# An attention and feed-forward kernel: pair 0's short pieces loaded alone, readers of later loads planned behind the landing with a margin, early squares and normalizations allowed on DVE

## The chip, the cores and the metric

The kernel runs on one core of one Trainium2 chip. The metric is the device time of one execution in microseconds (us); the kernel before takes 449.25 us, the median of three runs (449.05 to 450.95). The core's engines have queues of their own that run in order: TensorE (PE; its weight loads are shown as PEld), VectorE (DVE), ScalarE (ACT), GpSimd (POOL), and SyncE (SP), which here only issues transfers. An instruction that waits holds up all that stand behind it in its queue.

## The reference

Attention with normalized q and k over 8 batches, 12 heads, 448 positions and 64 channels, then a feed-forward layer over the 3584 tokens:

```python
def rmsnorm(x, g):
    rms = np.sqrt(np.mean(x * x, axis=-1, keepdims=True) + 1e-06)
    return x / rms * g

q_n, k_n = rmsnorm(q, g_q), rmsnorm(k, g_k)
scores = (1 / np.sqrt(64)) * np.matmul(q_n, k_n.transpose(0, 1, 3, 2))
scores = scores - np.max(scores, axis=-1, keepdims=True)
attn = np.exp(scores)
attn = attn / (np.sum(attn, axis=-1, keepdims=True) + 1e-09)
x = np.matmul(attn, v)                      # -> tokens x 768
h = x @ w_in                                # 768 x 2048
out = (h * np.clip(h + 3.0, 0.0, 6.0) / 6.0) @ w_out   # 2048 x 768
```

Inputs and output are float32.

## The kernel before

**Tiles and stages.** Work goes by pairs of heads: 48 pairs, six to a batch. The 448 positions of a head are three blocks of 128 and a rest of 64. The blocks are one "main" load (`load_main`, L323) of all the pairs that one call names; the rests of the two heads of a pair share one 128-row block, so that k and v need two "rest" transfers (`load_rest`, L331) and q one (L329). All go into rings of eight pairs, `qk_st` and `v_st`.

For each pair, with k as half 0 and q as half 1:

- `square` (L352 on ACT, L354 on POOL) writes `sq`; `sums` (L357, DVE) adds up 64 channels each into `ssq`; `rstd` (L363, L364, ACT) takes a logarithm and an exponential of half of it.
- `normalize` (L367, POOL or DVE) writes `qkn` in bf16 for one half.
- `transposes` (L383, PE), from pair 20 on a DMA transpose (L388, issued by SP), turns `qkn` into `qkT`; `put_q` (L395 on ACT, L397 on DVE) scales q by the product of g_q and g_k and 1/8, which `make_g` (L523, L525, DVE) makes out of two small loads (L520, POOL's queue); `put_k` is a copy (L334).
- `score` (L406, PE) fills a PSUM bank, `expo` (L416, ACT) makes `eR` (the rest block) or `eD` (a block of both heads): four exponentials for a pair. `weigh` (L429, PE) multiplies by v, which `cast_v` (L334) has put into `vaug` beside a column of ones; `divide` (L437, L438, DVE) makes `xn`, and `x_out` (L448, PE, or a DMA transpose, L452, from pair 18 on) with `put_x` (L459, DVE) makes `xT`.

For each batch whose six pairs are done, 16 input items of six matmuls (L462) follow, each with a `relu` (L468, ACT) and a `gate` (L473, DVE) that frees the item's PSUM bank; then output items of 16 matmuls (L481), a copy into `y_sb` (L334, DVE or ACT) and a store (L492 to L495, SP). Only two PSUM banks serve these items (four once the last pair is scored), so an input or output item waits for the gate or copy of the item two before it.

**Who sets the order.** The kernel is written out by a planner (`Plan`). It keeps a clock of its own with a duration for each operation and a model of the transfers, and at each step it takes, on each engine that is free, the ready operation with the lowest key (for most a pair's number and a rank). The order in which it emits is the order of each engine's queue on the chip; its times are only its own. What matters here:

- `Op.ways` lists the engines that may do an operation and a duration for each. `run` takes the way with the least of "engine free, plus duration times PRICE", so that a low price attracts work: POOL 0.5, ACT 2.0, DVE 1.5. Operations with a negative first key (those of pairs 0 and 1) have no price.
- A transfer counts as landed (`flow`) after DEPART (1000 ns), its planned size at a modelled rate, and LAND (1100 ns). `after` then sets the earliest planned time of its readers, HOP (60 ns) later. Past STEADY (60 us of planned time) a PE operation that waits for another engine is set SLACK (500 ns) later.
- `feed_forward` puts input and output items into two lanes, from which PE takes when its attention work has no credit or is not ready.

**The start.** For pair 0 the kernel loads the main blocks of pairs 0 and 1 one by one and the rests of pairs 0 to 3 in one go, k on SP's queue and q on ACT's; then k and q of pairs 2 and 3, then v. DVE's queue begins with memsets that clear the unused half blocks (`clear` L499 to L501, `clear_v` L504 and L505) and write ones (`ones`, L508 to L510), among which stands `make_g`; POOL makes the identity, loads g_q and g_k and fills `eR` and `eD`.

Of the kernel before, what the change touches and what calls it, by code (L numbers as in the profile page):

```python
# [44 lines left out]
class Plan:  # L45


    HOP = 60
    PRICE = {"POOL": 0.5, "ACT": 2.0, "DVE": 1.5}
    ISSUE, DEPART, LAND, BULK, DEPTH = 620, 1000, 1100, 0.64, 8  # L50
    STEADY, SLACK = 60e3, 500
    LAG = {"POOL": 45, "ACT": 105, "DVE": 85}
    UNITS = 4

# [16 lines left out]

    def dma(self, key, n, size, fn, deps=(), queue="SP", hold=False, issue=None):
        op = self.add(key, [(queue, (issue or self.ISSUE) * n, fn)], deps, self.LAND, size, hold)
        op.subs = n
        return op

    def dma_transpose(self, key, size, fn, deps):
        op = self.add(key, [("SP", 1270, fn)], deps, self.LAND, size)
        op.subs = 1
        return op  # L80

    def item(self, lane, place, count, ns, fn, deps, want):
# [58 lines left out]
    def after(self, op, engine, now):  # L141
        for n in op.next:
            n.left -= 1
            n.time = max(n.time, op.end + self.HOP)
            if engine != "PE" and now > self.STEADY and n.ways[0][0] == "PE":
                n.time = max(n.time, op.end + self.SLACK)
            if n.left == 0 and n.key is not None:
                self.known.append(n)
# [21 lines left out]
    def run(self):  # L170
        now = 0.0
        while self.todo or self.row or any(self.lanes.values()):
            self.flow(now)
            soon = [t for t in self.free.values() if t > now]
            t = self.rates(now)[1]
            if t is not None:
                soon.append(t)
            for ops in self.issued.values():
                soon += [x.end for x in ops[-3 * self.DEPTH:] if x.end is not None and x.end > now]
            best = {}  # L180
            for op in self.known:
                if op.time > now:
                    soon.append(op.time)
                    continue
                if op.calm is not None and (self.backlog("SP", "ACT") > op.calm[0] or self.backlog("POOL") > op.calm[1]):
                    continue
                engine, ns, fn = min(op.ways, key=lambda w: max(self.free[w[0]], now) + w[1] * (self.PRICE.get(w[0], 1.0) if op.key[0] >= 0 else 1.0))
                if self.free[engine] <= now and (engine not in best or op.key < best[engine][0].key):
                    if op.subs and not self.room(op, engine, now):
                        continue  # L190
                    banks = self.banks_for(op, now, soon) if op.want else None
                    if op.want is None or banks is not None:
                        best[engine] = (op, ns, fn, banks)
            if self.free["PE"] <= now and ("PE" not in best or self.credit < 0):
                if self.row:
                    best["PE"] = (self.row[0], *self.row[0].ways[0][1:], None)
                else:
                    pick = self.next_item(now, soon)
                    if pick:
                        it, banks = pick  # L200
                        for lane in self.lanes.values():
                            if lane and lane[0] is it:
                                lane.pop(0)
                        self.row = list(it.ops)
                        best["PE"] = (self.row[0], *self.row[0].ways[0][1:], banks)
            if not best:
                now = min(soon)
            for engine, (op, ns, fn, banks) in best.items():
                if op.key is None:
                    self.row.pop(0)  # L210
                    share = next((self.share[i] for i in range(0, len(self.share) - 1, 2)
                                  if it.place < self.share[i + 1]), self.share[-1])
                    self.credit = min(self.credit + ns * share, 2000.0)
                else:
                    self.known.remove(op)
                    self.todo -= 1
                    if engine == "PE":
                        self.credit = max(self.credit - ns, -2000.0)
                self.begin(op, engine, ns, fn, now, banks)
        return now  # L220
# [3 lines left out]
def kernel(  # L224
# [11 lines left out]
    nc = tc.nc  # L236
# [380 lines left out]
    YLAG, EARLY = 0.12, 1  # L617

    W_AFTER, LA, VL = 2, 4, 1.2
    MAIN_OF = {p: 2 for p in range(4, NPAIR, 2)}  # L620
    REST_OF = {p: 4 for p in range(4, NPAIR, 4)}
    w_ops = [plan.dma((-1, n), 1, 2830 if n < NWI else 4990, lambda n=n: load_w(n), queue="POOL", hold=True, issue=900)
# [35 lines left out]
    for p in range(NPAIR):  # L658
        if p == 0:
            lg = plan.dma((-3, 0), 2, 10, lambda: load_g(nc.gpsimd), queue="POOL", issue=900)  # L660
            for a, aq, qq in ((0, nc.sync, "SP"), (1, nc.scalar, "ACT")):
                load(a, 0, 1, 4, 0, aq, qq)
                load(a, 1, 1, 0, 0, aq, qq)
            add((1, 1.5), [("ACT", 1300, lambda: nc.scalar.preload_act_table_set("natural_log_exp_and_others"))])
            mg = add((-1, 0), [("DVE", 300, make_g)], [lg])
            load(0, 2, 2, 0, 0)
            load(1, 2, 2, 0, 0)
            load(2, 0, 2, 4, 2.5)
            lv = load(2, 2, 2, 0, 1.5)
            for w in w_ops:  # L670
                lv.next.append(w)
        elif p in REST_OF or p in MAIN_OF:
            for a in range(3):
                load(a, p, MAIN_OF.get(p, 0), REST_OF.get(p, 0), VL if a == 2 else 0)

# [5 lines left out]
        if p < NFAST:  # L681
            stats = []
            for a in range(2):
                s1 = add((p - 2, 2), [("POOL", 1000, lambda p=p, a=a, m=m: square(G, p, one[a], m)),
                                      ("ACT", 530, lambda p=p, a=a, m=m: square(A_, p, one[a], m))],
                         srcs[a] + sq_free + zeros)
                stats.append(s1)
            if p < 2:
# [12 lines left out]
            s2 = 2 * [add((p - 2, 0), [("ACT", 440, lambda p=p: rstd(p, both))], [s2])]  # L701
        norms[p] = []
        for a in range(2):
            ways = [("POOL", 1000, lambda p=p, a=a: normalize(G, p, a)), ("DVE", 1400, lambda p=p, a=a: normalize(V, p, a))]
            norms[p].append(add((p - 2, 4), ways[:2 if p < NFAST else 1], [s2[a], at(tr, p - NQ)]))
        vc.append(add((p, 5), [("DVE", 1350, lambda p=p: cast_v(V, p)),
                               ("POOL", 575, lambda p=p: cast_v(G, p)),
                               ("ACT", 530, lambda p=p: cast_v(A_, p))],
                      [*landed[2][p], at(clo, p), at(clv, p // 2), weighed.get(p - NV)]))
# [17 lines left out]
        def steps(todo, pairs=None):  # L727
# [16 lines left out]
            for n, (p, i) in enumerate(todo):  # L744
                scored.setdefault(p, []).append(op)
                old = weighed.get(p - NER) if i == NT else tile_of.get(NT * p + i - NED)
                e = add((p, 1), [("ACT", 790 if i < NT else 440, lambda p=p, i=i, c=cells[n]: expo(p, i, c["b"]))], [op, old])
                op.gives.append(e)
                k = count.get(p, 0)
                count[p] = k + 1  # L750
# [68 lines left out]
```

## Time and profile before

| | us |
|---|---|
| median of three runs | 449.25 |
| the profiled execution | 446.75 |
| its span from the first to the last instruction | 445.0 |
| span without a PE matmul | 30.9 |
| DVE waiting for ACT's relu (gate) | 88.1 |
| ACT waiting for a DMA transpose (put_q) | 15.6 |
| POOL waiting for a load of q (square) | 11.8 |
| DVE waiting for POOL's square (sums) | 23.6 |
| DVE waiting for PE's weighing (divide) | 24.5 |

The profile is of one execution. Times in its views are microseconds from the start of the span. A line of the timeline gives start, duration, engine, line of the kernel, operation, what is written and read, and in brackets how long the engine had been idle and what ended that. An idle engine costs time only where PE, which works 93% of the span, waits for it in the end. The granted clock of PE was full (0.998 in the mean).

The page's chain of the work that ended last gives PE 59%, DMA 14%, POOL 12%, DVE 5%.

### The profile page before, as it was taken

The page shows a single profiled execution, that of the slowest core. Times are in us where ns is not written, and L with a number is a line of the kernel's source. Part 1 is how long each engine was busy: PE and PEld are TensorE (multiplying, and loading weights), DVE is VectorE, ACT ScalarE, POOL GpSimd, SP SyncE. Part 2 cuts the span into 40 slices and gives each one's busy share as a digit, 9 for nine tenths or more (in the row PEclk, how much of TensorE's full clock was granted, in tenths as well). Part 3 has the DMA queues.
Part 4 walks back from the last instruction along what each step waited for, and adds up shares of the span by engine and source line. Part 5 has one row for each costly group of instructions (what it writes and reads, how often), then busy time and mean ns, then how long its engine had stood idle before and what let it go on. Part 6 is the DMA issues. An engine that isn't in the chain of part 4 may idle for free.

```text
span 445.0 us, 8973 instructions
## 1 busy us (share of the span) xinstructions
PE 414.1 (93%) x3576; PEld 235.5 (53%) x3576; DVE 226.0 (51%) x412; ACT 259.9 (58%) x479; POOL 213.7 (48%) x212
## 2 busy tenths in 40 slices
PE   0888998999999979999999989999999999999996
PEld 0555655555555435554555545555556555555563
DVE  6586887858544555355463454334334343343321
ACT  3899888875766858576876576656753032132100
POOL 6999999999657557393773472401000000000000
PEclk9999999999999999999999999999999999999999
DMA  8999999998799895985969755246212201100021
GB/s 218 265 247 249 229 171 228 233 245 135 176 191 203 182 173 99 231 205 133 179 156 202 189 126 97 50 70 108 72 24 60 84 1 48 60 38 36 37 72 71
DMA packets 117962, 62.20 MB, mean 140 GB/s; under 512 B 67232, under 2 KB 114336, under 8 KB 117920
## 3 DMA queue, kind: packets, MB, share of 16 engines
q1 hardware_dynamic: 106352, 54.81, 53.6%
q0 software_dynamic: 10496, 6.29, 10.3%
q10 hardware_dynamic: 1072, 0.52, 0.5%
q8 instruction: 28, 0.46, 0.4%
q14 instruction: 14, 0.11, 0.1%
HBM read 45.61 MB, written 11.01 MB: 127 GB/s over the span
## 4 chain that ended last, share of the span: by engine, by line
PE 59%; DMA 14%; POOL 12%; DVE 5%; SPq 3%; ACT 3%; issue 3%; POOLq 0%; ACTq 0%; DVEq 0%
PE ps L481 21%; PE ps L462 20%; DMA qk_st<-in_q_dram 8%; POOL sq L354 6%; PE av L429 5%; PE sc L406 5%; POOL qkn L367 5%; PE sc L481 4%; DMA qkT<-qkn 4%; DVE ssq L357 2%; PE sc L462 2%; DMA v_st<-in_v_dram 1%; SPq L331 1%; SPq L323 1%; DVE gT L473 1%
## 5 line engine op out<-in xcount | busy, mean ns | idle before, releaser
L462 PE MATMUL ps<-xT,w_in_sb 128*128 128x448 bf16 x726 | 166.4, 352 | 4.1 <-DVE gT L473 3.3
L481 PE MATMUL ps<-w_out_sb,gT 128*128 128x384 bf16 x784 | 147.1, 326 | 3.9 <-DVE gT L473 3.9
L416 ACT ACTIVATE eD<-sc 128x896 bf16<-128x896 f32 x144 | 127.2, 913 | 22.8 <-PE sc L406 15.6
L473 DVE SCALAR_TENSOR_TENSOR gT<-t_sb,ps 128x448 bf16<-128x448 f32 x121 | 74.6, 619 | 85.2 <-ACT t_sb L468 85.2
L481 PEld LDWEIGHTS <-gT 128*128 128x128 bf16 x896 | 82.0, 98 | 61.2 <-issue 13.4
L468 ACT ACTIVATE t_sb<-ps 128x448 f32<-128x448 f32 x121 | 65.6, 543 | 79.0 <-PE ps L462 77.2
L367 POOL TENSOR_TENSOR qkn<-qk_st,rstd 128x512 bf16<-128x512 f32 x95 | 97.4, 1046 | 14.1 <-DMA qkT<-qkn 9.6
L462 PEld LDWEIGHTS <-w_in_sb 128*128 128x128 bf16 x768 | 68.7, 97 | 63.0 <-issue 15.4
L354 POOL TENSOR_TENSOR sq<-qk_st 128x1024 f32<-128x1024 f32 (+1 forms) x47 | 82.6, 1765 | 19.4 <-DMA qk_st<-in_q_dram 11.8
L357 DVE TENSOR_REDUCE ssq<-sq 128x16 f32<-128x1024 f32 (+1 forms) x50 | 58.4, 1173 | 24.4 <-POOL sq L354 23.6
L406 PE MATMUL sc<-qkT 64*128 64x448 bf16 (+1 forms) x336 | 60.0, 360 | 5.0 <-ACT eD L416 2.5
L429 PEld LDWEIGHTS <-eD 128*128 128x128 bf16 x1152 | 52.8, 98 | 21.6 <-issue 4.7
L429 PE MATMUL av<-vaug,eD 128*128 128x65 bf16 x1152 | 58.8, 194 | 0.4 <-DVE xn L438 0.4
L334 POOL CAST vaug<-v_st 128x512 bf16<-128x512 f32 x37 | 22.6, 617 | 75.4 <-PE av L429 75.2
L334 DVE COPY y_sb<-ps 128x384 f32<-128x384 f32 x43 | 23.9, 555 | 54.4 <-PE ps L481 54.2
L438 DVE TENSOR_TENSOR xn<-av,rden 128x512 bf16<-128x512 f32 x48 | 33.2, 692 | 1.7
L416 ACT ACTIVATE eR<-sc 128x448 bf16<-128x448 f32 x48 | 26.0, 542 | 12.0 <-PE sc L406 11.7
L406 PEld LDWEIGHTS <-qkT 64*128 64x128 bf16 (+1 forms) x336 | 14.9, 95 | 32.6 <-issue 28.0
L395 ACT ACTIVATE qkT<-qkT,gprime 128x448 bf16<-128x448 bf16 x28 | 18.6, 665 | 15.7 <-DMA qkT<-qkn 15.6
L437 DVE RECIPROCAL rden<-av 128x8 f32<-128x8 f32 x48 | 9.8, 203 | 24.5 <-PE av L429 24.5
L383 PE MATMUL ps<-identity,qkn 128*128 128x128 bf16 x120 | 10.7, 237 | 11.8 <-POOL qkn L367 11.4
L481 PE MATMUL sc<-w_out_sb,gT 128*128 128x384 bf16 x112 | 19.3, 326 | 0.0
(50 smaller groups left out, 164.0 us busy)
## 6 DMA issues: line engine op xcount, KB each, us to landing
v_st<-in_v_dram SPq DMA_DIRECT2D x24, 384.0 KB, 6.5
out_dram<-y_sb SPq DMA_DIRECT2D x24, 384.0 KB, 2.5
qk_st<-in_k_dram SPq DMA_DIRECT2D x23, 384.0 KB, 5.7
qk_st<-in_q_dram SPq DMA_DIRECT2D x23, 384.0 KB, 6.2
w_in_sb<-in_moe_w_in_dram POOLq DMA_DIRECT2D x8, 384.0 KB, 9.4
w_out_sb<-in_moe_w_out_dram POOLq DMA_DIRECT2D x4, 768.0 KB, 10.5
qk_st<-in_k_dram SPq DMA_DIRECT2D x24, 64.0 KB, 5.3
v_st<-in_v_dram SPq DMA_DIRECT2D x24, 64.0 KB, 5.5
```

Of the source, the lines that this page charges most:

```text
L334: (eng.copy if eng is nc.scalar else eng.tensor_copy)(out=out, in_=in_)
L354: eng.tensor_tensor(out=sq, in0=x, in1=x, op=A_MULT)
L357: nc.vector.tensor_reduce(out=ssq_r[p % NR][:, a].rearrange("p a s -> p (a s)"), in_=sq_r[m % 2][:, a].rearrange("p a s d -> p (a s) d"), ...
L367: eng.tensor_tensor(out=qkn_r[p % NQ][:, a].rearrange("p t h d -> p h t d"), in0=qk_st[:, a, p % NS], in1=rstd_r[p % NR][:, a].rearrange(" ...
L406: nc.tensor.matmul(out=bank(u, h)[:, 0:S], lhsT=qkT[rows, 0, i * P:(i + 1) * P], rhs=qkT[rows, 1, 0:S], start=True, stop=True,)
L416: nc.scalar.activation(out=e[..., 0:S], in_=src[..., 0:S], func=EXP, bias=0.0, scale=1.0)
L429: nc.tensor.matmul(out=out, lhsT=e_tile(p, i, h)[:, c0:c0 + P], rhs=rhs, start=first and j % 2 == 0 and h == 0, stop=last, skip_group_chec ...
L438: nc.vector.tensor_tensor(out=xn_r[p % NQ][:].rearrange("p n (h d) -> p n h d", h=2), in0=av4[:, :, :, 0:D], in1=rden[:].unsqueeze(3).to_b ...
L462: nc.tensor.matmul(out=bank(m)[:, 0:S], lhsT=w_in_sb[:, kt, f * P:(f + 1) * P], rhs=xT[:, kt, b % NX, x_slot(b)], start=(kt == 0), stop=(k ...
L468: nc.scalar.activation(out=t[:], in_=bank(m)[:, 0:S], func=RELU, bias=0.5, scale=1.0 / 6.0,)
L473: nc.vector.scalar_tensor_tensor(out=gT[:, f, (b % 2) * S:(b % 2 + 1) * S], in0=t[:], scalar=1.0, in1=bank(m)[:, 0:S], op0=A_MIN, op1=A_MULT,)
L481: nc.tensor.matmul(out=bank(m)[:, 0:n], lhsT=gT[:, f, c0:c0 + P], rhs=w_out_sb[:, f, c:c + n], start=(f == 0), stop=(f == NFT - 1),)
```

## The change

Five things, all in the planner's tables and in the list of loads:

1. Pair 0's rests are loaded alone (k on SP, q on ACT), and the rests of pairs 1 to 3 after pair 1's main blocks, as transfers of their own; those of q go from ACT's queue to SP's.
2. After 60 us of planned time, the reader of a landed transfer is planned 3.5 us behind the landing of a load and 2.0 us behind that of a DMA transpose. These are planned times: on the chip the reader still waits for its own semaphores only.
3. Before 45 us of planned time the prices are other ones: POOL 0.7, ACT 1.5, DVE 0.9; and a square may go to DVE.
4. Planned durations: `normalize` on DVE 1200 instead of 1400 ns, `cast_v` on DVE 700 instead of 1350, an exponential 800 instead of 790.
5. The ranks of v's first loads get names, V0 and V2, with the values that they had.

```diff
-    PRICE = {"POOL": 0.5, "ACT": 2.0, "DVE": 1.5}
+    PRICE, FIRST, UNTIL = {"POOL": 0.5, "ACT": 2.0, "DVE": 1.5}, {"POOL": 0.7, "ACT": 1.5, "DVE": 0.9}, 45e3
-    STEADY, SLACK = 60e3, 500
+    STEADY, SLACK, LATE = 60e3, 500, {"load": 3500, "turn": 2000}
...
             n.time = max(n.time, op.end + self.HOP)
+            if engine == "DMA" and now > self.STEADY:
+                n.time = max(n.time, op.end + self.LATE["turn" if op.turn else "load"])
...
-                engine, ns, fn = min(op.ways, key=lambda w: max(self.free[w[0]], now) + w[1] * (self.PRICE.get(w[0], 1.0) if op.key[0] >= 0 else 1.0))
+                engine, ns, fn = min(op.ways, key=lambda w: max(self.free[w[0]], now) + w[1] * ((self.FIRST if now < self.UNTIL else self.PRICE).get(w[0], 1.0) if op.key[0] >= 0 else 1.0))
...
             for a, aq, qq in ((0, nc.sync, "SP"), (1, nc.scalar, "ACT")):
-                load(a, 0, 1, 4, 0, aq, qq)
-                load(a, 1, 1, 0, 0, aq, qq)
+                load(a, 0, 1, 1, 0, aq, qq)
+            load(0, 1, 1, 0, 0)
+            load(1, 1, 1, 0, 0, nc.scalar, "ACT")
+            load(0, 1, 0, 3, 0.2)
+            load(1, 1, 0, 3, 0.2)
...
                 s1 = add((p - 2, 2), [("POOL", 1000, lambda p=p, a=a, m=m: square(G, p, one[a], m)),
-                                      ("ACT", 530, lambda p=p, a=a, m=m: square(A_, p, one[a], m))],
+                                      ("ACT", 530, lambda p=p, a=a, m=m: square(A_, p, one[a], m)),
+                                      ("DVE", 1200, lambda p=p, a=a, m=m: square(V, p, one[a], m))],
...
-            ways = [("POOL", 1000, lambda p=p, a=a: normalize(G, p, a)), ("DVE", 1400, lambda p=p, a=a: normalize(V, p, a))]
+            ways = [("POOL", 1000, lambda p=p, a=a: normalize(G, p, a)), ("DVE", 1200, lambda p=p, a=a: normalize(V, p, a))]
...
-        vc.append(add((p, 5), [("DVE", 1350, lambda p=p: cast_v(V, p)),
+        vc.append(add((p, 5), [("DVE", 700, lambda p=p: cast_v(V, p)),
```

In `load(a, p, main, rest, rank)`, `a` is 0 for k, 1 for q, 2 for v, `main` and `rest` say how many pairs a transfer covers, and the rank is added to the pair's number in the key. `op.turn` is set in `dma_transpose` alone.

## The prediction

> **What bounds the kernel now.** I read the page's head first, then the engines in windows of 10 us, then the timeline of the start, then TensorE's waits one by one. The head:
>
> ```profile
> span 445.0 us, 8973 instructions
> ...
> PE 414.1 (93%) x3576; PEld 235.5 (53%) x3576; DVE 226.0 (51%) x412; ACT 259.9 (58%) x479; POOL 213.7 (48%) x212
> ```
>
> TensorE (PE) is the bound: 445.0 - 414.1 = 30.9 us without a matmul row is all that a schedule can win. The three runs have a median of 449.25 us; the profiled execution took 446.75, so my sum against the profile is carried to the median by adding 2.5.
>
> Where the idle time lies, by windows (columns: stretch, sum; busy us and instructions of PE, PEld, DVE, ACT, POOL; granted clock; DMA share; GB/s):
>
> ```profile
> 0.00:10.00 10.00, 0.00 (x0) 0.00 (x0) 6.07 (x36) 3.17 (x7) 6.30 (x24) 1.00 0.82 214
> 10.00:20.00 10.00, 8.24 (x64) 4.76 (x66) 5.98 (x10) 8.24 (x20) 10.00 (x12) 1.00 1.17 250
> 20.00:30.00 10.00, 8.41 (x130) 5.87 (x126) 7.02 (x16) 9.62 (x18) 9.83 (x12) 1.00 1.21 269
> 30.00:40.00 10.00, 8.99 (x110) 5.64 (x111) 6.94 (x14) 9.56 (x18) 9.97 (x11) 1.00 1.25 257
> 40.00:50.00 10.00, 9.16 (x97) 5.32 (x95) 8.01 (x15) 9.09 (x20) 9.96 (x10) 1.00 1.22 239
> ```
>
> Three parts. First, PE starts at 10.69. Second, the first input matmul comes at 37.26, so until then, and mostly until 50 us, only attention feeds PE, and ACT and POOL are full; PE loses 1.76 + 1.59 + 1.01 + 0.84 = 5.2. Third, from 60 to 345 us PE waits singly: its timeline shows 17 gaps of 0.25 to 2.64 us, 10.9 in all. From 345 us on the same output and input matmuls stand in the same order in both programs; nothing is to be had there.
>
> The start (DVE, then POOL, then PE):
>
> ```profile
> 6.71 0.15 DVE L523 TENSOR_TENSOR gprime<-gq_t,gk_t 64x1 f32<-64x1 f32 x1 [1.54 <-DMA gk_t<-in_g_k_dram]
> ...
> 8.04 0.27 DVE L501 MEMSET qk_st<- 64x256 f32 x1
> ...
> 8.34 2.47 DVE L357 TENSOR_REDUCE ssq<-sq 128x8 f32<-128x512 f32 x4
> ...
> 9.59 3.49 POOL L367 TENSOR_TENSOR qkn<-qk_st,rstd 128x512 bf16<-128x512 f32 x3 [1.44 <-ACT rstd L364]
> ...
> 10.69 0.61 PE L383 MATMUL ps<-identity,qkn 128*128 128x128 bf16 x4 [10.69 <-POOL qkn L367]
> ```
>
> The first sums stand on DVE behind make_g, which waited for the g_k transfer until 6.71, and behind six memsets. The last square of pair 0 (ACT, 7.34 to 7.95) was ready before DVE was.
>
> The largest gap of the third part, on POOL, DVE, ACT and PE:
>
> ```profile
> 158.12 1.89 POOL L354 TENSOR_TENSOR sq<-qk_st 128x1024 f32<-128x1024 f32 x1 [2.62 <-DMA qk_st<-in_q_dram]
> ...
> 160.05 1.22 DVE L357 TENSOR_REDUCE ssq<-sq 128x16 f32<-128x1024 f32 x1 [2.77 <-POOL sq L354]
> ...
> 159.18 0.67 ACT L395 ACTIVATE qkT<-qkT,gprime 128x448 bf16<-128x448 bf16 x1 [1.34 <-DMA qkT<-qkn]
> ...
> 161.85 0.97 PE L481 MATMUL ps<-w_out_sb,gT 128*128 128x384 bf16 x5 [2.64 <-DVE gT L473]
> ```
>
> A late load holds POOL's square, this holds the sum at the head of DVE's queue, and behind the sum stands the gate that frees PE's bank. A late DMA transpose does the same through put_q at the head of ACT's queue. I looked at ACT and DVE around each gap: behind late loads lie 0.80 (150 us), 2.64 (162), 1.05 (259) and 0.45 (263), together 4.9; behind late transposes 0.34 (156), 0.77 (191), 0.44 (223), 0.79 (295) and 0.25 (309), together 2.6. The other 3.4 have other causes.
>
> **The change, part by part.**
>
> *Short pieces of pair 0.* The square of pair 0 can start earlier, but the sum cannot: in the changed order DVE still has make_g ahead of it, and two more memsets (L504 and L505 of the last slots, moved from POOL; 0.23 + 0.17 from their starts at 4.77 and 5.00). From the first sum to PE the profile has 10.69 - 8.34 = 2.35. So PE starts 0.4 later, near 11.1. Behind that, SP issues three more transfers ahead of the loads of pair 2 (two k rests at 0.76, one q rest at 0.60: 2.1 us), and ACT's put_q of pair 0 now stands behind two more squares, one of pair 2. With q of pair 2 issued at 4.81 + 2.1 and landing 6.2 later it may be 13.1 before that square runs, while transposes would end near 12.8: up to 0.8 more. Bounds +0.4 and +1.2; I take +0.8, as both lags meet on ACT's one queue.
>
> *Squares and normalizations on DVE.* By the order of the whole program DVE gains one square, five normalizations, three casts of v and two memsets, and loses one put_q and one put_k before the first gate. POOL loses five normalizations and three casts and gains two half squares; ACT loses three squares and a cast and gains a put_q and a put_k early: -3 x 0.61 - 0.62 + 0.63 + 0.59 = -1.2. The two-input rows on DVE and POOL:
>
> ```profile
> L367 POOL TENSOR_TENSOR qkn<-qk_st,rstd x95: 1032/1042/1490, 9.6 to 287.5; 128x512 bf16<-128x512 f32 x95
> ...
> L367 DVE TENSOR_TENSOR qkn<-qk_st,rstd x1: 1183/1183/1183, 11.0 to 11.0; 128x512 bf16<-128x512 f32 x1
> ```
>
> DVE: 6 x 1.18 + 3 casts at 0.74 (no row; the 128x384 f32 copy of 0.555 scaled to 512; bounds 0.42, the bf16 copy, and 1.18) + 0.4 - 0.45 - 0.42 = 8.8 us more. It is hidden in DVE's idle time from 10 to 50 us, 4.0 + 3.0 + 3.1 + 2.0 = 12.1; without that cover it costs up to 8.8, since divide and put_k, which PE waits for, queue behind. POOL: -5 x 1.05 - 3 x 0.62 - 0.4 + 2 x 1.04 = -5.4. But the one POOL normalization that met the DVE one took 1.49 instead of 1.04, so six such meetings give back 6 x 0.45 = 2.7. No wait of PE between 20 and 50 us names POOL; I take nothing for POOL (bounds -2.7 and 0). ACT is the fuller one behind PE's waits there (eD, 2.1 us); I take half its relief, -0.6 (bounds -1.2 and 0).
>
> The Trainium skill, SBUF — State Buffer, section "Who interferes with whom", says that a DVE instruction with two SBUF inputs excludes a GpSimd one that reads SBUF, for its whole length, whichever came first. The 1.49 and the 1.18 (against 0.69 for the divide, whose one input is PSUM) agree. By that rule each of the six would cost POOL its unblocked length, near 0.69 as an estimate from the divide, 4.1 together, and the relief of 5.4 shrinks to 1.3; the sum, which takes nothing for POOL, stays.
>
> *The margin.* It adds no instruction. After 60 us of planned time the planner puts readers of loads 3.5 us and of transposes 2.0 us behind the planned landing. Planned from issue to landing, without a queue: q main 1.0 + 1.16 + 1.1 = 3.3, transpose 1.0 + 1.6 + 1.1 = 3.7. Measured:
>
> ```profile
> qk_st<-in_q_dram SPq DMA_DIRECT2D x23, 384.0 KB, 6.2
> ...
> qkT<-qkn SPq DMA_TRANSPOSE x28, 4.4
> ```
>
> The loads are 2.9 late and POOL's longest wait for one is 3.2, both inside 3.5; ACT's waits at the gaps are 1.2 to 2.9, mostly inside 2.0. The order confirms that something moves: of the sums of pairs 20 to 47, 23 of 28 stand one divide later, and 22 of 28 put_q one to three exponentials later. Nobody starves by it: those sums still run 5 to 11 pairs ahead of the divide and put_q 3 to 7 exponentials ahead of its own pair. So 4.9 x 23/28 + 2.6 x 22/28 = 6.1 goes, less 1.1 (a third of the 3.4 of other gaps) for new meetings in a new order: -5.0. Bounds -7.5, all of it, and -1.5, when most waits only move.
>
> Rounded durations and V0, V2 change only choices that the order above already has: nothing, by that order.
>
> Sum: +0.8 - 0.6 - 5.0 = -4.8. Profiled 446.75 - 4.8 = 442.0; median 444.5, by its own bounds (+0.4 - 1.2 - 7.5 to +1.2 - 1.5) 441 to 449.
>
> **Rivals.**
> 1. *The waits only move.* PE's credit with the feed-forward lanes is the same, and a gate that no longer waits behind a sum may wait behind an exponential. For: 3.4 us of gaps already have such causes. Against: the depth of 5 to 11 pairs. Only 1.5 comes back: 449.25 + 0.8 - 0.6 - 1.5 = 448.0.
> 2. *DVE becomes the bound before 50 us* (slower). Its 8.8 us more, with POOL and DVE holding each other up, fall on the chain transposes, put_k, score, exponential, weigh, divide, and the first input matmul comes later by as much. For: DVE would be busy (27.95 + 8.8) / 40 = 92%, in order, and POOL is at 98 to 100%, so every two-input pair meets. Against: it needs all of the idle 12.1 us to be unusable; DVE waited 5.5 us there for the weighing before a divide, when it could have worked. It decides once DVE's share from 10 to 50 us passes about 9.5 tenths. 449.25 + 0.8 + 8.8 - 5.0 = 453.9.
> 3. *Everything pays*: g_k lands 0.5 sooner (g_q took 3.8, g_k 4.3), ACT's full 1.2 and all 7.5: 449.25 + 0.4 - 0.5 - 1.2 - 7.5 = 440.5.
> 4. *The pieces do what they say*, and PE starts before 10.69: this needs make_g moved, and the order has it where it was; within 3.
>
> **Chances.** Forecast 0.55, waits only move 0.20, DVE bound 0.13, everything pays 0.10, none of these 0.02. A difference under 0.5%, 2.2 us, is no change that this measurement can tell (the runs before spread over 1.9). The forecast lies past -2.2 in about 0.51 of its 0.55, the third rival wholly, the first in a tenth: faster 0.63. The first rival gives most of "same", 0.20; the second and half of what is left give slower, 0.17. Range 440 to 451.5: from the third rival past the first, with the second's centre outside; the likeliest case's own is 441 to 449.
>
> **What would show it.** First transposes at 11.0 to 12.0 (before 10.69: make_g was no bar). DVE between 10 and 50 us near 37 of 40, and its two-input rows near 1.18. POOL's waits for q loads, 11.8 us in all, under 3; ACT's for DMA transposes, 15.6, under 6; PE's gaps from 60 to 345 us 6, not 10.9. I am wrong if these gaps stay while POOL's waits go, or if the last exponential of pair 5 ends more than 3 us later than now (ACT's 24th, at 37.5).

## The result and the profile after

The changed kernel takes 447.3 us (median of 22 executions, 442.59 to 448.36) against 449.29 us (22 executions of the kernel before, 446.53 to 452.58). The ratio is 0.9932, with a 95% interval of 0.9905 to 0.9959: 3.05 us faster, where 4.8 was forecast. That is the ratio of the means; the two medians lie only 2.0 apart. The executions of the changed kernel lie in two groups, five at 442.6 to 443.2 and seventeen at 446.4 to 448.4. The profiled one (448.29 us) is of the second group, so it stands 1.5 above the profiled one of the kernel before (446.75), and what follows compares stretches of the two, not their ends. TensorE's mean granted clock is 0.996 in each of the five and 0.980 to 0.987 in the seventeen.

The head of the page of the changed kernel:

```profile
span 446.5 us, 9002 instructions
...
PE 415.3 (93%) x3576; PEld 235.9 (53%) x3576; DVE 243.0 (54%) x421; ACT 259.6 (58%) x478; POOL 211.1 (47%) x204
```

PE's idle time, 446.5 - 415.3 = 31.2 us, is what it was (30.9). That is two large changes that cancel, as the windows show. First the stretch that the margin was meant for, 60 to 345 us, of the kernel before and of the changed one (columns as in the windows above: stretch, sum; busy us and instructions of PE, PEld, DVE, ACT, POOL; granted clock; DMA share; GB/s):

```profile
60.00:345.00 285.00, 273.51 (x2507) 153.27 (x2504) 149.18 (x253) 195.23 (x353) 157.71 (x139) 1.00 0.73 152
```

```profile
60.00:345.00 285.00, 281.12 (x2630) 158.14 (x2629) 158.70 (x270) 202.59 (x369) 166.25 (x147) 1.00 0.71 154
```

PE is busy 7.6 us longer in the same 285 us, with 123 more matmuls done: here the change pays. The waits behind it, of the changed kernel (engine, line, what it waited for: us in all, times, longest):

```profile
PE ps L464 <- DVE xT L461: 5.9, 1, 5.9
POOL sq L356 <- DMA qk_st<-in_q_dram: 5.7, 4, 3.0
...
ACT qkT L397 <- DMA qkT<-qkn: 0.3, 1, 0.3
```

POOL's waits for q loads fell from 11.8 to 5.7, ACT's for DMA transposes from 15.6 to 0.3. The first of these lines, one wait of 5.9 us, is new. The windows of the changed kernel up to 60 us show where it lies:

```profile
0.00:10.00 10.00, 0.00 (x0) 0.00 (x0) 6.59 (x38) 2.90 (x6) 4.93 (x21) 1.00 0.67 182
10.00:20.00 10.00, 7.80 (x64) 4.38 (x64) 8.90 (x10) 8.92 (x22) 9.41 (x11) 1.00 1.16 261
20.00:30.00 10.00, 7.00 (x99) 4.34 (x96) 9.76 (x14) 8.33 (x17) 9.96 (x11) 0.97 1.19 268
30.00:40.00 10.00, 8.90 (x113) 6.48 (x112) 9.10 (x19) 9.23 (x17) 9.03 (x9) 0.86 1.23 264
40.00:50.00 10.00, 4.47 (x52) 2.39 (x49) 9.79 (x7) 5.14 (x10) 9.98 (x8) 0.82 1.16 234
50.00:60.00 10.00, 9.00 (x65) 5.07 (x65) 5.89 (x11) 4.23 (x10) 1.55 (x3) 0.67 0.63 136
```

From 10 to 50 us PE is busy 28.2 us (before 34.8) and DVE 37.6 of 40. From 40 to 50 us DVE shows seven instructions in 9.79 busy us. The timeline of the changed kernel names them (start, duration, engine, line, operation; in brackets the idle time before it and what ended it; POOL, DVE and PE):

```profile
41.72 0.88 POOL L348 DMA_DIRECT2D w_in_sb<-in_moe_w_in_dram  x1
42.62 4.04 POOL L369 TENSOR_TENSOR qkn<-qk_st,rstd 128x512 bf16<-128x512 f32 x4
46.62 3.73 POOL L356 TENSOR_TENSOR sq<-qk_st 128x1024 f32<-128x1024 f32 x2
50.31 0.86 POOL L348 DMA_DIRECT2D w_in_sb<-in_moe_w_in_dram  x1
...
43.78 6.86 DVE L336 CAST vaug<-v_st 128x512 bf16<-128x512 f32 x1
50.56 0.38 DVE L461 COPY xT<-ps 128x448 bf16<-128x448 bf16 x1
...
51.00 2.40 PE L464 MATMUL ps<-xT,w_in_sb 128*128 128x448 bf16 x6 [5.86 <-DVE xT L461]
```

One cast of v on DVE lasted 6.86 us, while POOL ran four normalizations and two squares one after the other; it ended as POOL turned to a DMA issue at 50.31. Behind it in DVE's queue stood the 0.38 us copy that writes x^T, and PE waited for that copy. The other two casts show what the same instruction costs otherwise (count: least, median, longest ns):

```profile
L336 DVE CAST vaug<-v_st x3: 537/831/6862, 35.2 to 50.9; 128x512 bf16<-128x512 f32 x3
...
L369 DVE TENSOR_TENSOR qkn<-qk_st,rstd x6: 693/1479/3030, 12.0 to 36.5; 128x512 bf16<-128x512 f32 x6
```

The longest of the normalizations, 3.03 us, is a smaller case of the same kind: PE waited 1.77 us for it (DVE, PE).

```profile
25.82 3.03 DVE L369 TENSOR_TENSOR qkn<-qk_st,rstd 128x512 bf16<-128x512 f32 x1
...
28.91 0.40 PE L385 MATMUL ps<-identity,qkn 128*128 128x128 bf16 x4 [1.77 <-DVE qkn L369]
```

And the start of the changed kernel (ACT, POOL, DVE, PE), for the first step of the prediction:

```profile
5.53 1.04 POOL L356 TENSOR_TENSOR sq<-qk_st 128x512 f32<-128x512 f32 x1 [1.16 <-DMA qk_st<-in_q_dram]
5.71 0.88 DVE L525 TENSOR_TENSOR gprime<-gq_t,gk_t 64x1 f32<-64x1 f32 x1 [0.56 <-DMA gk_t<-in_g_k_dram]
...
8.33 1.21 DVE L359 TENSOR_REDUCE ssq<-sq 128x8 f32<-128x512 f32 x2
9.51 3.52 POOL L369 TENSOR_TENSOR qkn<-qk_st,rstd 128x512 bf16<-128x512 f32 x3 [2.94 <-ACT rstd L366]
10.61 0.61 PE L385 MATMUL ps<-identity,qkn 128*128 128x128 bf16 x4 [10.61 <-POOL qkn L369]
```

g_k landed 1.0 sooner, and make_g's two-input instruction then met POOL's square (5.53 to 6.57) and took 0.88 instead of 0.15. The sum started at 8.33 (before 8.34) and PE at 10.61 (before 10.69).

### The profile page after: what moved, and what is told of

Same layout as the page of the kernel before. It is cut to its first block, busy times and chain, and to the rows that moved or that the text cites. A ratio compares the mean times of both kernels' runs of the same rounds, so it can differ in the third digit from the quotient of the medians.

```text
span 446.5 us, 9002 instructions
## 1 busy us (share of the span) xinstructions
PE 415.3 (93%) x3576; PEld 235.9 (53%) x3576; DVE 243.0 (54%) x421; ACT 259.6 (58%) x478; POOL 211.1 (47%) x204
## 4 chain that ended last, share of the span: by engine, by line
PE 69%; POOL 10%; DVE 7%; DMA 7%; issue 3%; SPq 2%; ACT 1%; POOLq 0%; DVEq 0%; ACTq 0%
PE ps L483 25%; PE ps L464 23%; PE av L431 6%; PE sc L408 6%; PE sc L483 5%; POOL qkn L369 5%; DMA qk_st<-in_q_dram 5%; POOL sq L356 4%; DVE ssq L359 2%; DVE vaug L336 2%; PE sc L464 2%; DMA qkT<-qkn 1%; DVE gT L475 1%; SPq L333 1%; DMA gk_t<-in_g_k_dram 1%
## 5 line engine op out<-in xcount | busy, mean ns | idle before, releaser
L464 PE MATMUL ps<-xT,w_in_sb 128*128 128x448 bf16 x732 | 169.2, 355 | 7.9 <-DVE xT L461 5.9
L483 PE MATMUL ps<-w_out_sb,gT 128*128 128x384 bf16 x752 | 141.4, 326 | 1.2 <-DVE gT L475 1.1
L369 POOL TENSOR_TENSOR qkn<-qk_st,rstd 128x512 bf16<-128x512 f32 x90 | 93.6, 1059 | 26.9 <-ACT rstd L366 16.8
L356 POOL TENSOR_TENSOR sq<-qk_st 128x1024 f32<-128x1024 f32 (+1 forms) x49 | 85.8, 1761 | 7.2 <-DMA qk_st<-in_q_dram 5.7
L431 PE MATMUL av<-vaug,eD 128*128 128x65 bf16 x1152 | 59.9, 195 | 0.0
L336 POOL CAST vaug<-v_st 128x512 bf16<-128x512 f32 x34 | 20.8, 618 | 77.6 <-PE av L431 77.6
L483 PE MATMUL sc<-w_out_sb,gT 128*128 128x384 bf16 x144 | 25.5, 326 | 0.0
L385 PEld LDWEIGHTS <-qkn 128*128 128x128 bf16 x160 | 11.1, 106 | 17.0 <-POOL qkn L369 11.9
L431 PE MATMUL av<-vaug,eR 128*128 128x130 bf16 x192 | 19.2, 224 | 0.0
```

The source lines that it names most:

```text
L336: (eng.copy if eng is nc.scalar else eng.tensor_copy)(out=out, in_=in_)
L356: eng.tensor_tensor(out=sq, in0=x, in1=x, op=A_MULT)
L369: eng.tensor_tensor(out=qkn_r[p % NQ][:, a].rearrange("p t h d -> p h t d"), in0=qk_st[:, a, p % NS], in1=rstd_r[p % NR][:, a].rearrange(" ...
L431: nc.tensor.matmul(out=out, lhsT=e_tile(p, i, h)[:, c0:c0 + P], rhs=rhs, start=first and j % 2 == 0 and h == 0, stop=last, skip_group_chec ...
L464: nc.tensor.matmul(out=bank(m)[:, 0:S], lhsT=w_in_sb[:, kt, f * P:(f + 1) * P], rhs=xT[:, kt, b % NX, x_slot(b)], start=(kt == 0), stop=(k ...
L483: nc.tensor.matmul(out=bank(m)[:, 0:n], lhsT=gT[:, f, c0:c0 + P], rhs=w_out_sb[:, f, c:c + n], start=(f == 0), stop=(f == NFT - 1),)
```

## The experiments

The theory: the margin earns what the windows show, and one DVE cast held by POOL, with the x^T copy behind it, gives most of it back. The rivals: the margin earns nothing and the early part is what pays; DVE is simply full; POOL's run of instructions needs only a pause. Ratios are to the kernel before on the same chip.

**The margin alone.** The kernel before with the changed kernel's margin and nothing else.

```diff
+    STEADY, SLACK, LATE = 60e3, 500, {"load": 3500, "turn": 2000}
...
+            if engine == "DMA" and now > self.STEADY:
+                n.time = max(n.time, op.end + self.LATE["turn" if op.turn else "load"])
```

> The kernel before with the margin alone (3.5 us behind loads, 2.0 behind DMA transposes, after 60 us of planned time); the first 60 us as before. If the margin does what the forecast says, TensorE's gaps of over 0.15 us between 60 and 345 us fall from 10.9 to 3 to 5 us, its gaps before 60 us stay at 10.7 + 4.4, and the time is 449.3 - 6.5 = 442.8 (441.5 to 444.5). Rival, the waits only move: gaps of 9 to 11 us and 448 to 450.

Measured: 437.59 us (436.75 to 438.31), ratio 0.9754 (0.9729 to 0.9778), 4 us below the expected range. Its window from 60 to 345 us:

```profile
60.00:345.00 285.00, 281.71 (x2564) 158.77 (x2565) 150.31 (x252) 197.43 (x357) 158.84 (x141) 1.00 0.73 154
```

The stretch is as good as the changed kernel's; PE's gaps over 0.15 us in it add up to 3.0 us, where the kernel before has 10.9 and the changed one 3.4. Up to 60 us it is the kernel before (first transposes at 10.81, PE busy 44.65 from 10 to 60 us against 44.80). So the margin by itself is worth 11.0 us (2.46% of 449.25; 9.7 between the two profiled spans, 445.0 and 435.3), and the rest of the change loses 8.

**The change without the margin.**

```diff
-    STEADY, SLACK, LATE = 60e3, 500, {"load": 3500, "turn": 2000}
+    STEADY, SLACK, LATE = 60e3, 500, {"load": 0, "turn": 0}
```

> The changed kernel with a margin of zero; the same order up to 60 us of planned time. If the margin earned what the changed kernel earns, the gaps between 60 and 345 us are 9 to 12 us again, the DVE cast of v near 44 us is still the long one (about 7 us in the slow executions), and the time is 447.3 + 7 = 454 (452 to 455.5). Rival, the early part earned it: 447 to 449.

Measured: 452.51 us (450.4 to 456.4), ratio 1.0094 (1.0063 to 1.0125), slower than before. In its profile the gaps from 60 to 345 us are back at 10.8, and a DVE cast took 6.87 with a gap of 5.87 on PE behind it. The early part of the change costs time by itself; by the ratios the margin earns 1.0094 - 0.9932 = 1.62%, 7.3 us, on top of it. That is less than the 11.0 that it earns alone, so what each part is worth depends on the order in which they are added.

**The casts of v on ACT.** The changed kernel's order, but the casts planned for DVE are issued on ACT.

```diff
-        vc.append(add((p, 5), [("DVE", 700, lambda p=p: cast_v(V, p)),
+        vc.append(add((p, 5), [("DVE", 700, lambda p=p: cast_v(A_, p)),
```

> The changed kernel in its own planned order, but the three casts of v that DVE does are issued on ACT instead. Theory of the port: the cast of 6.86 us near 44 us was held out by eight POOL instructions in a row that read SBUF; on ACT it takes 0.6, no gap of TensorE between 40 and 52 us is over 1.5 us, and all executions lie at 441 to 444. Rival, the cast waits for v itself (SP issues v's loads some 2 us later than before): ACT waits there instead, the gap of about 6 us stays, 447 us.

Measured: 439.94 us (439.7 to 440.51), ratio 0.9808 (0.9782 to 0.9833), a little below the expected range. The same place in its timeline (ACT, DVE, PE):

```profile
44.12 0.62 ACT L336 CAST vaug<-v_st 128x512 bf16<-128x512 f32 x1
...
44.56 0.39 DVE L461 COPY xT<-ps 128x448 bf16<-128x448 bf16 x1 [0.49 <-PE ps L450]
...
45.18 1.30 PE L464 MATMUL ps<-xT,w_in_sb 128*128 128x448 bf16 x6
```

The gap is gone. The same six matmuls take 1.30 us where the changed kernel has 2.40: there they come after 5.9 us of idle time, and the clock shows why. Windows of the changed kernel in steps of 2 us:

```profile
44.00:46.00 2.00, 1.14 (x11) 0.62 (x12) 2.00 (x1) 1.63 (x3) 2.00 (x3) 1.00 1.12 217
46.00:48.00 2.00, 0.00 (x0) 0.00 (x0) 2.00 (x1) 0.00 (x0) 2.00 (x2) 0.61 1.35 204
48.00:50.00 2.00, 0.00 (x0) 0.00 (x0) 2.00 (x1) 0.00 (x0) 2.00 (x2) 0.50 1.14 333
50.00:52.00 2.00, 1.00 (x3) 0.41 (x3) 1.40 (x3) 0.00 (x0) 1.17 (x2) 0.50 1.11 331
...
54.00:56.00 2.00, 2.00 (x26) 1.78 (x24) 0.92 (x2) 1.39 (x2) 0.00 (x0) 0.50 0.78 109
56.00:58.00 2.00, 2.00 (x18) 1.07 (x16) 2.00 (x4) 0.37 (x1) 0.00 (x0) 0.83 0.00 0
58.00:60.00 2.00, 2.00 (x18) 1.23 (x16) 1.57 (x4) 1.91 (x7) 0.37 (x1) 1.00 0.00 0
```

The clock fell to a half during the gap and stayed there until about 56.7. From the six matmuls to the second group of eight transposes behind them PE takes 7.62 us here (51.00 to 58.62) and 5.16 with the casts on ACT (45.18 to 50.34). The held cast thus costs 5.86 + 2.46 = 8.3 in this execution, and the two profiled spans differ by 446.5 - 438.4 = 8.1. The six executions of this kernel make one group (0.8 us wide), all at a mean granted clock of 0.995 or 0.996: with the casts off DVE the two groups were not seen. By the ratios the casts on DVE cost 0.9932 - 0.9808 = 1.24%, 5.6 us, over both groups of the changed kernel.

The clock also says something of the five quicker executions of the changed kernel. In the profiled one the granted clock of the 10 us windows lies below 1.00 by 0.03 + 0.14 from 20 to 40 us, as with the casts on ACT (0.05 + 0.13), and by 0.18 + 0.33 from 40 to 60 us, behind the held cast. As estimates from these windows, the first loss alone makes a mean of 0.996 over the span, and both together 0.985. The five have 0.996, so the loss behind the held cast is most likely missing in them. By their mean of 442.9, against 449.5 for the kernel before, they are still some 2 us slower than with the casts on ACT, so a shorter hold may be left.

**A pause between POOL's normalizations.** If a DVE instruction gets its turn whenever POOL changes operation, a one-column memset behind each early normalization should free it.

```diff
+    gap = const.tile([P, 1], FP32, name="gap")
...
+        if eng is nc.gpsimd and p < 16:
+            eng.memset(gap[:], 0.0)
```

> The changed kernel with a memset of one column after each of POOL's normalizations of pairs 0 to 15: an instruction that reads nothing, about 0.1 us each. If DVE gets its turn as soon as POOL's run of reading instructions is broken, the cast near 44 us takes at most 2 us, DVE's normalizations (0.69 to 3.03, median 1.48) come under 1.6, and the time is 442 to 444 in all executions. Rival, DVE needs an idle POOL or a DMA issue: the cast stays at 4 to 7 us and the time at 447 to 448.5.

Measured: 446.89 us (442.73 to 448.06, in two groups again), ratio 0.9963 (0.9936 to 0.9990). POOL and DVE in its timeline:

```profile
43.32 0.11 POOL L376 MEMSET gap<- 128x1 f32 x1
43.38 1.04 POOL L370 TENSOR_TENSOR qkn<-qk_st,rstd 128x512 bf16<-128x512 f32 x1
...
43.50 7.02 DVE L337 CAST vaug<-v_st 128x512 bf16<-128x512 f32 x1
...
44.36 0.10 POOL L376 MEMSET gap<- 128x1 f32 x1
...
50.18 0.87 POOL L349 DMA_DIRECT2D w_in_sb<-in_moe_w_in_dram  x1
```

The cast started inside one normalization and was still held past the memset at 44.36 and those behind it, until POOL issued a DMA. A short POOL instruction in between did not release it here.

**The cast by itself.** A test of its own: one DVE cast or normalization against nothing, against eight POOL normalizations, against eight POOL casts, and against POOL normalizations broken in the middle by a DMA issue or by a wait for ACT.

```diff
+    def phase(kind, op, brk=None, n=8):
+        G.tensor_copy(out=mark[0][:], in_=mark[2][:])
+        V.tensor_copy(out=mark[1][:], in_=mark[0][:])
+        op()
+        V.tensor_copy(out=mark[2][:], in_=mark[1][:])
+        run_of(n, kind, brk)
```

> Only a test of the port; nothing of the attention or the feed-forward is computed. POOL runs eight instructions in a row while DVE starts one cast of v or one normalization under the first of them; each phase three times. Theory, the cast never gets in between two POOL instructions that read SBUF: behind eight normalizations (1.04 each) it takes 7 to 9 us, and with a DMA issue or a wait for ACT after the fourth it takes 3.5 to 5; alone 0.54 to 0.85. DVE's normalization gets in after one or two of them: 1.2 to 2.7; alone 0.69. Rival, the 6.86 us had another cause: the cast takes at most 2 us in all phases.

Measured, alike in three repeats: alone, the cast takes 0.42 and the normalization 0.68; started in the first of POOL's eight normalizations 1.18 and 1.44, held to the end of one POOL instruction and no longer; under POOL casts 0.73 and 0.99; with the DMA issue in the middle 1.18; in the run after that one, broken by the wait for ACT, 4.18, to the end of all four POOL instructions ahead of the wait. The theory's 7 to 9 behind eight normalizations did not come, and the rival's limit of 2 did not hold either. So both outcomes exist, and the number of POOL instructions does not decide between them. One of the three held casts (POOL, DVE):

```profile
54.71 4.03 POOL L363 TENSOR_TENSOR qkn<-qk_st,rstd 128x512 bf16<-128x512 f32 x4
54.85 4.18 DVE L330 CAST vaug<-v_st 128x512 bf16<-128x512 f32 x1
```

**By the place of the start, and by a DMA issue before.** The same test with the DVE instruction started later and later in POOL's run, once without and once with two DMA issues by POOL just before the run.

```diff
+        if before:
+            before()
+            G.tensor_copy(out=mark[0][:], in_=mark[2][:])
...
+        for _ in range(off):
+            V.tensor_copy(out=mark[3][:], in_=mark[1][:])
```

> Only a test of the port; nothing of the attention or the feed-forward is computed. A cast or a normalization on DVE starts at several places under POOL's run of eight normalizations, with and without a DMA issue by POOL just before the run; runs broken by a wait for ACT stand at both ends. Theory one, the place decides: some starts give 1.0 to 1.6 and others 4 to 8.5, alike with and without the DMA issue. Theory two, POOL's DMA issue decides: without it all casts take at most 1.6, behind it 4 or more. Theory three, the later wait of POOL decides: only the runs broken by the wait for ACT hold the cast, for their first four instructions (4.2).

Measured: of 19 DVE instructions in runs with no DMA issue by POOL just ahead, none was held beyond one POOL instruction (0.42 to 1.44). Of nine in runs behind a DMA issue, the first three casts, which started inside POOL's first instruction, were short (1.19, 0.84, 0.47). The other three casts, started in its second instruction or later, and all three normalizations, the first of them started at the very beginning of the run, were held to the run's end (7.04, 6.66, 6.28; 8.42, 7.67, 6.92). After that, without a DMA issue, again 1.18 and 1.44. A short and a held cast, and one held normalization:

```profile
49.58 8.22 POOL L363 TENSOR_TENSOR qkn<-qk_st,rstd 128x512 bf16<-128x512 f32 x8
49.73 1.17 DVE L330 CAST vaug<-v_st 128x512 bf16<-128x512 f32 x1
...
154.39 0.52 POOL L516 DMA_DIRECT2D gk_t<-in_g_k_dram  x1
155.04 8.03 POOL L363 TENSOR_TENSOR qkn<-qk_st,rstd 128x512 bf16<-128x512 f32 x8
156.33 7.04 DVE L330 CAST vaug<-v_st 128x512 bf16<-128x512 f32 x1
...
184.84 8.42 DVE L363 TENSOR_TENSOR qkn<-qk_st,rstd 128x512 bf16<-128x512 f32 x1
```

In the changed kernel POOL had issued a w_in DMA at 41.72, and the cast started in the second normalization behind it. That agrees with the held casts of the test. The normalization of 3.03 us fits too: POOL had issued a DMA at 22.18, and it started in POOL's fourth instruction behind that. So none of the three theories holds as it was put: behind a DMA issue the place of the start decided for the casts of this test, while the normalizations were held from every place. What in the DMA issue brings it about the runs don't show.

**The two halves of the margin.** The kernel before with the margin for loads alone, and with that for DMA transposes alone.

```diff
+    STEADY, SLACK, LATE = 60e3, 500, {"load": 3500, "turn": 0}
```

> The kernel before with the margin behind loads alone (3.5 us), none behind DMA transposes. By the forecast's split, 4.9 us of gaps behind loads against 2.6 behind transposes, two thirds of what the whole margin earned (449.3 to 437.6 against the same kernel before) come from the loads: 448.5 - 0.65 x 10.6 = 441.6 (439.5 to 443.5). Rival, transposes matter more, since an exponential behind put_q holds all that follows: 444 or more.

```diff
+    STEADY, SLACK, LATE = 60e3, 500, {"load": 0, "turn": 2000}
```

> The kernel before with the margin behind DMA transposes alone (2.0 us), none behind loads. Loads alone earned 5.6 us (443.5 against 449.0) and the whole margin about 11. If the two add up, this takes 449 - 5 = 444 (442.5 to 445.5). Rival, they overlap, one removed wait being enough at most places: 440 to 442. Rival, the transposes' margin helps only where readers of loads are late too: 447 or more.

Measured: loads alone 443.49 us (442.93 to 443.88), ratio 0.9883 (0.9860 to 0.9906), -5.3 us of 449.25; transposes alone 440.82 us (439.68 to 442.23), ratio 0.9816 (0.9786 to 0.9846), -8.3 us. With loads alone POOL's waits for q loads fall to 0.8 and ACT's for transposes rise to 20.7; with transposes alone POOL's are 15.8. The two sum to 13.6, more than the 11.0 of both together, as the second expectation's first rival has it. The gaps don't show this overlap: PE's gaps from 60 to 345 us are 6.8 with loads alone and 7.2 with transposes alone, 4.1 and 3.7 less than before, which add up to the 7.9 that both remove. Whether the halves overlap stays open.

**The short pieces alone**, on the kernel before with the margin.

```diff
-                load(a, 0, 1, 4, 0, aq, qq)
-                load(a, 1, 1, 0, 0, aq, qq)
+                load(a, 0, 1, 1, 0, aq, qq)
+            load(0, 1, 1, 0, 0)
+            load(1, 1, 1, 0, 0, nc.scalar, "ACT")
+            load(0, 1, 0, 3, 0.2)
+            load(1, 1, 0, 3, 0.2)
```

> The kernel before with the margin and with pair 0's short pieces, without the early prices, the square on DVE and the new durations. Margin alone took 437.6; margin, pieces and early DVE work with the casts on ACT 439.9. If the pieces are hidden behind make_g, as the forecast says, TensorE's first transposes stay within 0.6 us of 10.7 and the time lies within 1.5 of the margin alone: 436.5 to 439. Rival, the pieces cost the 2.3 us (v's loads issued some 2 us later): 439.5 to 441.

Measured: 436.27 us (436.08 to 436.57), ratio 0.9722 (0.9700 to 0.9744). First transposes at 10.46, 0.35 sooner than with the margin alone. The median is 1.3 lower than that kernel's, but on another chip, and the intervals of the ratios overlap: the pieces cost nothing and may gain a little.

**The early prices without the pieces**, with the casts issued on ACT.

```diff
-                load(a, 0, 1, 1, 0, aq, qq)
-            load(0, 1, 1, 0, 0)
-            load(1, 1, 1, 0, 0, nc.scalar, "ACT")
-            load(0, 1, 0, 3, 0.2)
-            load(1, 1, 0, 3, 0.2)
+                load(a, 0, 1, 4, 0, aq, qq)
+                load(a, 1, 1, 0, 0, aq, qq)
...
+        vc.append(add((p, 5), [("DVE", 700, lambda p=p: cast_v(A_, p)),
```

> The changed kernel with the loads of the kernel before (no pieces), its margin and early prices, and the casts that DVE would do issued on ACT. If the early squares and normalizations on DVE cost the 2.3 us (normalizations of 1.5 to 3 us on DVE that transposes wait for), the time is 439 to 442 and TensorE has a gap of over 1 us behind a DVE normalization between 20 and 40 us. Rival, the pieces cost it: 437 to 438.5.

Measured: 440.51 us (439.4 to 440.97), ratio 0.9809 (0.9787 to 0.9832); by the ratios 2.5 us slower than the margin alone. PE is busy 41.62 from 10 to 60 us against 44.65, mostly lost from 10 to 30 us (14.73 against 16.55). But only three normalizations went to DVE here, none over 1.53 us, and no gap above 1 us stands behind one. So the early prices, with the square on DVE and the new durations, cost some 2.5 us even with no cast on DVE, and no single wait names their cause. The expected gap behind a DVE normalization did not come, though the time lies in the expected range.

**make_g behind pair 0's sums**, on the margin with the pieces.

```diff
-            mg = add((-1, 0), [("DVE", 300, make_g)], [lg])
...
+                if p == 0:
+                    mg = add((-1, 0), [("DVE", 300, make_g)], [lg, *s2])
```

> Margin and pieces (436.3), and make_g planned behind the sums of pair 0 on DVE. If make_g's wait for g_k is what holds the first sums, they begin near 6.7 instead of 8.3, TensorE's first transposes come at 8.7 to 9.5 instead of 10.5, and the time falls by 0.7 to 1.5, to 434.8 to 435.6. Rival, the pieces themselves or ACT's queue hold pair 0: first transposes at 10 or later and 436 to 437.

Measured: 435.8 us (435.18 to 436.97), ratio 0.9709 (0.9679 to 0.9739), 0.2 us above the expected range. DVE and PE at its start:

```profile
6.54 1.26 DVE L359 TENSOR_REDUCE ssq<-sq 128x8 f32<-128x512 f32 x2
7.71 0.14 DVE L525 TENSOR_TENSOR gprime<-gq_t,gk_t 64x1 f32<-64x1 f32 x1
...
8.87 0.61 PE L385 MATMUL ps<-identity,qkn 128*128 128x128 bf16 x4 [8.87 <-POOL qkn L369]
```

PE starts 1.59 sooner than with the pieces alone (10.46), which shows that make_g was the bar. The median, on another chip, falls by only 0.5, which the intervals don't tell from nothing; part of the start is given back later, for instance in a gap of 1.30 at 71.7 us in which PE waits for a w_in transfer. This kernel has the lowest median of all, 13.1 us under the kernel before by its ratio and 10 under the changed one.

## Why the prediction was right and wrong

The sign and the range held. The median of 447.3 lies inside the forecast's own 441 to 449, but as the sum of two errors of opposite sign, which is luck. It is also close to what the first rival gave (448.0), for a reason that is not the first rival's. By ratios of 449.25: margin -11.0, early prices and pieces with the casts off DVE +2.4, casts on DVE +5.6, together -3.0. Each ratio has an interval of about 1.1 us to either side, and another order of adding the parts gives other sizes (the margin 7.3 instead of 11.0).

*The margin, forecast -5.0, bound -7.5: right mechanism, too small.* Loads and transposes that held the heads of DVE's and ACT's queues were the cause of most of the gaps, and with the margin alone the gaps went from 10.9 to 3.0. Of these 3.0, four gaps up to 78 us (1.8) stand in both kernels, and four of 0.26 to 0.33 us (1.2) stand behind that, two of them near places where the kernel before has gaps behind late transposes (0.34 and 0.44). So nearly all of the 7.5 behind late readers went, and the factors 23/28 and 22/28, by the share of instructions that had moved, took off 1.4 that was not lost. Of the 3.4 with other causes another 1.5 went, which the forecast had not counted. The 1.1 for new meetings was not far off: at most 1.2 is new. Together the gaps give 7.9 of the 9.7 between the profiled spans; 1.3 more is PE's busy time (414.1 to 412.8). That the ratio gives 11.0 fits the profiled execution of the kernel before (446.75), which is faster than its median. Of the split, 4.9 for loads and 2.6 for transposes, the runs give 5.3 and 8.3 by the ratios and 4.1 and 3.7 by the gaps: the part of the transposes was put too low.

*Squares, normalizations and casts on DVE, forecast "hidden in DVE's idle time": this step failed.* It priced a cast at 0.74, bounds 0.42 and 1.18. Those are right when a cast runs alone or meets one POOL instruction (0.42, 0.73, 1.18 in the test), but the bound "one POOL instruction" was taken from the single meeting that the profile before showed. The held cast took 6.86, and a normalization 3.03. The step also summed DVE's idle time over 40 us and did not ask what stands directly behind each new instruction: behind this one stood the x^T copy, for which PE had nothing else to do. And it did not count what a gap of this length does to the clock, another 2.5 us. DVE's busy share came out where forecast, 37.55 of 40 against "near 37", but that too is luck: 6.86 of it is the held cast, which takes 0.42 alone. The normalizations have a median of 1.48 where 1.18 was taken. POOL's normalizations that met a DVE one took the 1.49 of the forecast (at 19.75 us in the changed kernel). The -0.6 for ACT's relief was not seen: PE lost time from 10 to 30 us, also with the casts on ACT.

The Trainium skill, SBUF — State Buffer, section "Who interferes with whom", says that whoever issues first keeps the shared ports for its whole instruction and the other engine blocks. The 1.18, 1.44 and 1.49 agree with that; the 6.86 and the six held rows of the test go beyond it, since there DVE lost to the whole rest of POOL's run.

*The start, forecast +0.8: the bar was right, the size wrong.* make_g did bar the sum, as the last experiment shows. But g_k landed 1.0 sooner (the third rival alone had counted on that, with 0.5), and make_g's meeting with POOL's square took 0.73 of it back: -0.1 instead of +0.8. The prediction's own sign, that a start before 10.69 means that make_g was no bar, misled: PE started at 10.61, and make_g was the bar all the same.

*Rival 2, "DVE becomes the bound before 50 us", had the place and not the mechanism.* DVE at 94% just misses its point of decision, 95%. Had a full DVE been the cause, taking three casts (0.54 to 0.83 each, but one held) off it would have earned some 2 us; it earned 8.1 in the profiled spans, from one of them. Rival 1 fell: 10.9 us of gaps became 3.4, the waits did not just move.

*The other signs.* POOL's waits for q loads stayed at 5.7 where under 3 was named, but PE's gaps fell to 3.4, below the 6 that was named, and ACT's waits for transposes to 0.3. The last exponential of pair 5 ended at 39.3, 1.8 later than before and within the 3 that would have told against the forecast. The cast that was held started at 43.78, behind that point, so this sign could not catch it.

*Left open.* How long the cast was held in the five executions at 442.6 to 443.2: their clock speaks against the long hold, but the profile is of the other group. Where the 2.4 us go that the early part costs besides the casts: the 1.77 us wait for the held normalization is there with the casts on ACT too (1.8), but the kernel without the pieces has no such wait and loses as much. What in a DMA issue by POOL makes it hold DVE afterwards.

## What to carry to other kernels

A reader of a transfer at the head of an in-order queue should stand behind the measured landing (6.2 us here) and not behind the planned one (3.3); in this kernel that one line of the planner, alone, was worth 2.5%, while the rest of the change lost time. Before an instruction is moved to DVE, look at what POOL runs at that time and at what stands next in DVE's queue: an operation of 0.4 us lasted as long as the rest of POOL's run, and whatever waits behind it waits as long. A change of several parts that comes out near nothing should be taken apart, since here its best part alone is 8 us faster than the whole.

## What the hardware showed that was not expected

A DVE cast or two-input instruction was held by POOL over one instruction in some meetings (1.18, 1.44) and to the end of POOL's run in others (4.18 over four, 6.86 over the rest of six, 8.42 over eight). The long ones were seen only after POOL had issued a DMA, just ahead of the run or in the run before; not every meeting after a DMA issue was long. A POOL memset of 0.1 us did not free the cast; POOL's next DMA issue (50.31), its wait or the end of the run did. The normalization of 3.03 us ended only at 28.85, 1.2 behind the start of POOL's next DMA issue at 27.62.

An idle TensorE of 5.9 us came back at a granted clock of 0.50 and needed about 5.7 us of work (51.0 to 56.7) to return to 1.00. The Trainium skill, TensorE: Matmul & The Clock Gate, Part 1 ("The HAM clock gate"), gives a full clock after about 3.4 us of sustained work; the measured return took longer.

Shorter idle times went with a lower clock too: from 26 to 30 us PE was busy 2.17 of 4, with the gap of 1.77, and from 30 to 32 us the clock was 0.50. With the casts on ACT it was the same (1.95 of 4, then 0.50). The windows of the changed kernel:

```profile
26.00:28.00 2.00, 1.08 (x19) 0.68 (x15) 2.00 (x1) 1.70 (x5) 2.00 (x3) 1.00 1.28 219
28.00:30.00 2.00, 1.09 (x8) 0.34 (x8) 2.00 (x3) 0.66 (x2) 1.98 (x3) 0.85 1.29 231
30.00:32.00 2.00, 1.70 (x18) 1.58 (x17) 1.97 (x4) 2.00 (x3) 2.00 (x2) 0.50 1.18 265
```
